# First attention pairs finished segment by segment, routing and low halves spread over a shared port, and two more raw buffers for early weight loads

## The chip, the cores and the metric

The kernel runs on one core of one Trainium2 chip. The metric is device time in microseconds (us) of one execution of the whole program, as the median of several runs. The core's engines are TensorE (PE in the rows, its weight loads PEld), VectorE (DVE), ScalarE (ACT), GpSimd (POOL) and SyncE (SP). Here SP does nothing but issue DMA transfers, in one fixed order.

## The reference

Attention with pooled queries feeds a mixture of experts with two experts for each row:

```
q_pool = q.reshape(B, H, S // 2, 2, D).mean(axis=3)      # B, H, S, D = 4, 8, 1152, 64
scores = matmul(q_pool, k.T) / sqrt(D)
attn   = exp(scores - max) / (sum + 1e-9)
x      = (attn @ v) laid out as 2304 rows of 512
noisy  = x @ w_gate + log1p(exp(x @ w_noise)) * noise    # 8 experts
top2   = the two largest of each row; weights = softmax of them
out    = sum over top2 of weight * (relu(x[mask] @ w1[e]) @ w2[e])   # 512 -> 1024 -> 512
```

All inputs and outputs are float32. The kernel keeps that precision by splitting numbers into a high and a low 16-bit half and multiplying the halves separately.

## The kernel before

**Attention.** The 32 heads (4 batches, 8 heads) are taken as 16 pairs. Each pair has 9 chunks of 128 queries, which make three segments of 3 chunks, so there are 48 segments. The score work is cut into 216 units `u` of two blocks of 128 keys by 384 queries. A unit goes through four engines: PE multiplies (`score`, L349 and L350), ACT takes the exponential (`exp`, L357), VectorE or GpSimd computes the low half of P (`p_lo`: one 128x768 instruction on VectorE, L362, or two of 128x384 on GpSimd, L365), and PE multiplies by V (`pv`, L385). Six P buffers (`pt`) connect these steps.

Before a pair's scores can run, its row maxima must be known. For each chunk PE makes two products against half of the keys (`max_mm`, L304), ACT takes a relu (L312), and VectorE a maximum (L318). For each segment a rest product and its maximum follow (`max_rest`, `rest_red`, L327). `max_fin` (three small VectorE instructions, L334 to L336) puts the negated maximum into two columns of `qn2`, and SP transposes `qn2` into `qt2` by DMA (L294). Pair 0 does this last step for each segment. All other pairs do it once, after their ninth chunk. The transposed queries `qt` (from `qn`) and keys `kt` (from `kn`) come by the same kind of DMA, and `kd` is a VectorE difference of transposed keys (L298).

**Routing.** The first half of the rows is complete when 8 pairs are done. Its routing (`Route.steps`) is a chain of PE logits (L693), some sixty small VectorE instructions on the tiles `rta` and `rua` (the softplus, the two largest, and the place of each row in its expert's list), and 18 scatters by GpSimd to `xg` in device memory (L97). The second half is routed in three parts when attention ends.

**Experts.** While attention ends, SP transposes 256 rows of each of the experts 0 and 1 out of `xg` (tile `xe`), and these are multiplied early (`Moe.early`). The weights come through four raw buffers that attention no longer needs (`kr`, `qr`, `kn`, `vr`); ACT and VectorE split them into halves (`split`, L918 and L920). From about 510 us on, the remaining products of all eight experts run (`Moe.run`).

**What sets the order.** Attention and the early products are written out by a list scheduler, class `Plan`. Every operation has an engine, a cost, a key (its due place, in blocks of attention), dependences and buffers. The scheduler takes, on the engine that can start first, the operation with the smallest key among those that start within `WIN` = 0.25 of the earliest. `port=True` keeps operations of VectorE and GpSimd from overlapping in the plan. The plan sets only the order of the instructions on each engine; on the chip they wait for each other by semaphores, and each engine, SP too, takes its instructions in that order.

Of the kernel before, what the change touches and what calls it, by code (L numbers as in the profile page):

```python
# [62 lines left out]
LATE = 440  # L63

# [47 lines left out]
class Plan:  # L112
# [64 lines left out]
    def run(s):  # L177
        while s.hard or s.holds:
            at = {}
            for o in s.can:  # L180
                b = s.start(o)
                if b is not None:
                    at.setdefault(b[1], []).append((b[0], o.key, o, b[2]))
            pick = None
            for e, c in at.items():
                m, _, _, cost = min(c, key=lambda x: (x[0], x[1]))
                lim = m + (WIN if s.soft else cost / 4)
                x = min((x for x in c if x[0] <= lim), key=lambda x: (x[1], x[0]))
# [12 lines left out]
            o.done = st + cost + (s.LAT[e] if o.lat is None else o.lat)  # L201
            s.now = st
            s.hard -= o.gen is None
            o.fn(e) if len(o.eng) > 1 else o.fn()
            for tag in o.give:
                s.end[tag] = max(s.end[tag], o.done)
                s.refs[tag] -= 1
                if not s.refs[tag]:
                    s.pools[s.home[tag]].append([s.end[tag], s.buf.pop(tag)])
            for x in o.succ:  # L210
                x.ready = max(x.ready, o.done)
            for x in o.succ + o.then:
                x.wait -= 1
                if not x.wait:
                    s.can.append(x)


class Attn:
# [95 lines left out]
    def max_red(s, i, c):  # L314
        if i not in s.mx:
            s.mx[i] = s.sm.tile([P, NCQ, 2], F32, name="mx")
        rd = s.G.buf["rd", i, c]
        s.nc.vector.tensor_tensor_reduce(out=rd, in0=s.G.buf["S", i, c], in1=rd, scale=1.0, scalar=-3.0e38,  # L318
                                         op0=ALU.add, op1=ALU.max, accum_out=s.mx[i][:, c, 0:1])

    def max_rest(s, i, g):
        kt, ps = s.G.buf["kt", i], s.G.buf["R", i, g]
# [86 lines left out]
    def pairs(s):  # L409
# [8 lines left out]
        for i in range(NPAIR):  # L418
# [16 lines left out]
            for h, c in enumerate(hs):  # L435
# [13 lines left out]
            for p in ((0, 1) if x else (2,)):  # L449
# [13 lines left out]
                t = op("SP", 1.35, k(43, 91) + 8 * p * x, lambda i=i, c=c: s.transpose(B["qt", i][:, c], B["qn", i][:, c]), deps=[hi], lat=2.7,  # L463
# [5 lines left out]
            allred = []  # L469
            for g in range(3):  # L470
# [14 lines left out]
                rest = op("PE", 0.39 if g == 1 else 0.17, k0 + 5, lambda i=i, g=g: s.max_rest(i, g), deps=red, take=[("bank", ("R", i, g))])  # L485
                red.append(op("DVE", 0.47, k0 + 7, lambda i=i, g=g: s.rest_red(i, g), deps=[rest], give=[("R", i, g)]))
                allred += red
                if x or g == 2:
                    c = slice(3 * g, 3 * g + 3) if x else slice(0, NCQ)
# [3 lines left out]
                           lat=3.0, take=[("qt2", ("qt2", i))] if g == 0 or not x else (), give=[("qn2", i)], after=ready[0, 0][0] if x and g else None)  # L493
                    for y in ((g,) if x else (0, 1, 2)):
# [12 lines left out]
        for u in range(NU):  # L507
# [5 lines left out]
            pls[u] = op((("POOL", 1.43), ("DVE", 0.87)), 0, 2 * u + 2, lambda eng, u=u: s.p_lo(u, eng), deps=[ex[u]], port=True)  # L513
        for n in range(NSEG):
            i, g = SEQ[n]
            done = []
            for kc in range(NK):
                t = n * NK + kc
                done.append(op("PE", 0.375 if g == 1 else 0.28, t + 8, lambda n=n, kc=kc: s.pv(n, kc), deps=[pls[t // 2]] + vdone[i], after=done[-1] if done else None,
# [6 lines left out]
    def others(s, F0, out):  # L526
# [3 lines left out]
        op("DVE", 1.2, 112, R.setup1, deps=[a], ready=30.0)  # L530
# [23 lines left out]
        s.route(R.steps(0, (0, 1, 2), R.A, 0.8), 245, [s.ev[i, g] for i in range(NH) for g in range(3)], 3.0, then=then, pace=0.8)  # L554
# [23 lines left out]
    def route(s, gen, key, deps, slack, soft=False, then=None, pace=0.0, first=("SP", 1.35)):  # L578
# [8 lines left out]
        def piece(bank, held):  # L587
# [9 lines left out]
            wait, eng, cost = d if isinstance(d, tuple) else (0.0, "DVE", 0.12 if soft else 0.3)  # L597
            ready = G.now + (0.24 if soft else 0.4) + wait + (slack if eng == "PE" else 0.0)
# [6 lines left out]
            else:  # L605
                add(eng, cost, ready=ready)
# [11 lines left out]
class Route:  # L618
# [14 lines left out]
    def setup0(s):  # L633
        nc = s.nc
        wg, wn, noise = s.args
# [5 lines left out]
        nc.gpsimd.iota(s.tok, pattern=[[P, 2 * NCQ]], base=1, channel_multiplier=1, allow_small_or_imprecise_dtypes=True)  # L641
        s.wf = s.wk.tile([P, 4, 2 * E], F32, name="wf", bufs=1)
# [56 lines left out]
    def steps(s, j, gs, tag, gap, L=None):  # L699
# [166 lines left out]
class Moe:  # L866
# [27 lines left out]
    def load(s, eng=None):  # L894
# [5 lines left out]
        r = s.B.flat(s.F0.raws[(s.nl - 1) % 4])  # L900
# [102 lines left out]
    def early(s, A):  # L1003
# [4 lines left out]
        s.W[0, "1"] = s.F0.w  # L1008
        fl, ld, done = {}, {}, {}
# [15 lines left out]
        for x, (e, nm) in enumerate(((0, "2"), (1, "1"), (1, "2"))):  # L1025
            for c in range(4):
                key = LATE + (2, 12, 24)[x] + (2, 2.5, 2.5)[x] * c
                hi = op("ACT", 1.06, key, lambda e=e, nm=nm, c=c: s.split(e, nm, c, 0), deps=[ld[x, c]] if x else ())
                lo = op("DVE", 1.14, key, lambda e=e, nm=nm, c=c: s.split(e, nm, c, 1, False), deps=[hi])
                last = ld[x + 1, c] = op("SP", 0.6, key, s.load, deps=[lo], lat=5.0, after=last)  # L1030
                done.setdefault((e, nm), []).append(lo)
        done[0, "1"] = [A.f0]
        for e in range(2):
# [178 lines left out]
```

## Time and profile before

| what | us |
|---|---|
| median of 3 runs (range) | 890.33 (889.83 to 892.76) |
| the profiled execution | 896.5 |
| its span in the trace | 894.6 |
| PE busy in the span | 819.0 (92%) |
| VectorE busy | 534.6 (60%) |
| ACT busy | 445.0 (50%) |
| GpSimd busy | 402.6 (45%) |

All times of rows come from the profiled execution. Attention ends at about 446 us, the early products run from there to about 510 us, and the main expert products from there to the end. Busy shares are averages over these stages, and they hide where one engine waits for another, so the rows below are read by stage. [...]

### The profile page before, as it was taken

Reading aid. Unit: us, or ns where it says so; the run is one execution under the profiler, and the core shown is the slowest. Engines: PE = TensorE matmul, PEld = TensorE weight load, DVE = VectorE, ACT = ScalarE, POOL = GpSimd, SP = SyncE. Lnnn points to the kernel's source line nnn. Section 1 sums busy time; section 2 is a strip of 40 time slices with the busy share of each in tenths; the row PEclk is TensorE's granted clock in tenths of the full one; section 3 lists DMA queues with packets and bytes.
Section 4 is the critical chain, followed back from the end, with each engine's and each line's share of the span. In section 5 each row is a group of like instructions: output and inputs, shape, how many; then the busy total and the mean of one; then the engine's idle time right before and its main releaser. Section 6 shows DMA issues by size and latency. Waiting matters only on the chain.

```text
span 894.6 us, 21128 instructions
## 1 busy us (share of the span) xinstructions
PE 819.0 (92%) x8685; PEld 537.1 (60%) x8685; DVE 534.6 (60%) x1226; ACT 445.0 (50%) x662; POOL 402.6 (45%) x389
## 2 busy tenths in 40 slices
PE   3889999999999877899988899999999999999995
PEld 1546777767767655677766365756475655647542
DVE  4877898899889988899887142434233241422200
ACT  4658888777878465586543132333233232322310
POOL 4447879887996867664633312020201102020222
PEclk9989999999999779899989899999999999999998
DMA  8899796898999587664586826282827346291143
GB/s 194 166 238 211 181 231 176 200 200 194 194 214 203 116 183 189 169 172 110 122 215 231 205 55 147 82 214 71 217 68 201 84 126 158 72 219 18 24 52 45
DMA packets 213637, 137.80 MB, mean 154 GB/s; under 512 B 150304, under 2 KB 183584, under 8 KB 213536
## 3 DMA queue, kind: packets, MB, share of 16 engines
q1 hardware_dynamic: 204896, 116.33, 53.6%
q0 software_dynamic: 8640, 20.08, 11.0%
q8 instruction: 69, 1.13, 0.5%
q14 instruction: 32, 0.26, 0.1%
HBM read 62.14 MB, written 35.44 MB: 109 GB/s over the span
## 4 chain that ended last, share of the span: by engine, by line
PE 64%; DVE 20%; issue 4%; ACT 4%; DMA 3%; another core or an unknown queue 1%; SPq 1%; POOL 1%; ACTq 0%; DVEq 0%; POOLq 0%
PE pss L971 23%; PE psm L988 21%; PE psm L385 7%; PE psm L304 5%; PE pss L350 4%; DVE pl L362 4%; PE pss L349 4%; DVE rd L318 3%; DVE kd L298 1%; ACT rd L312 1%; ACT pf L357 1%; DVE vv L288 1%; DVE mx L327 1%; DMA qt<-qn 1%
## 5 line engine op out<-in xcount | busy, mean ns | idle before, releaser
L365 POOL TENSOR_TENSOR pl<-pf 128x384 f16<-128x384 f32 x288 | 279.9, 1002 | 95.6 <-ACT pf L357 70.9
L357 ACT ACTIVATE pf<-pss 128x768 f32<-128x768 f32 x216 | 174.2, 813 | 72.1 <-PE pss L350 59.1
L97 POOL DMA_INDIRECT out_dram<-y,mti x40 | 62.2, 1554 | 317.4 <-ACT y L993 311.8
L385 PEld LDWEIGHTS <-pf 128*128 128x128 bf16 x2880 | 159.6, 99 | 52.8 <-issue 23.7
L385 PE MATMUL psm<-vv,pf 128*128 128x65 f16 (+1 forms) x2880 | 169.9, 196 | 6.0 <-ACT rd L312 3.2
L385 PE MATMUL psm<-vv,pl 128*128 128x65 f16 (+1 forms) x1440 | 161.1, 195 | 4.5 <-DVE pl L362 2.9
L349 PE MATMUL pss<-qt,kt 128*128 128x384 f16 (+1 forms) x576 | 152.1, 293 | 5.6 <-ACT pf L357 5.4
L350 PE MATMUL pss<-qt,kt 66*128 66x384 f16 (+1 forms) x576 | 152.6, 294 | 0.4 <-DMA qt<-qn 0.4
L981 DVE SCALAR_TENSOR_TENSOR hl<-pss,hh 128x640 f16<-128x640 f32 (+1 forms) x64 | 48.5, 758 | 158.9 <-ACT hh L980 158.9
L385 PEld LDWEIGHTS <-pl 128*128 128x128 f16 x1440 | 128.6, 100 | 6.1 <-DVE pl L362 3.4
L988 PE MATMUL psm<-wh,hh 128*128 128x512 f16 x320 | 122.5, 383 | 3.8 <-ACT hh L1015 3.8
L988 PE MATMUL psm<-wh,hl 128*128 128x512 f16 x320 | 122.3, 382 | 0.5 <-issue 0.5
L988 PE MATMUL psm<-wl,hh 128*128 128x512 f16 x320 | 122.5, 383 | 0.1
L318 DVE CUSTOM_DVE_ANT_0 rd<-psm,rd 128x512 f32<-128x512 f32 x144 | 97.3, 684 | 25.4 <-ACT rd L312 21.0
L988 PEld LDWEIGHTS <-hh 128*128 128x128 f16 x640 | 62.9, 98 | 79.8 <-ACT hh L1015 4.6
L993 ACT ACTIVATE y<-psm,mg 128x512 f32<-128x512 f32 x40 | 27.5, 688 | 152.0 <-issue 77.3
L980 ACT ACTIVATE hh<-pss 128x640 f16<-128x640 f32 (+1 forms) x64 | 41.7, 652 | 122.9 <-PE pss L971 122.9
L312 ACT ACTIVATE rd<-psm 128x512 f32<-128x512 f32 x144 | 85.9, 597 | 24.6 <-PE psm L304 19.7
L304 PE MATMUL psm<-kt,qt 128*128 128x512 f16 (+3 forms) x320 | 79.8, 325 | 16.4 <-DVE mx L318 8.7
L971 PE MATMUL pss<-xT,fh 128*128 128x320 f16 (+1 forms) x448 | 83.4, 303 | 0.0
L971 PE MATMUL pss<-xT,wh 128*128 128x320 f16 (+1 forms) x448 | 83.4, 303 | 0.0
L362 DVE TENSOR_TENSOR pl<-pf 128x768 f16<-128x768 f32 x72 | 82.0, 1151 | 0.2 <-ACT pf L357 0.2
(198 smaller groups left out, 1141.3 us busy)
## 6 DMA issues: line engine op xcount, KB each, us to landing
xg<-zt SPq DMA_DIRECT2D x40, 260.0 KB
kr<-in_k_dram SPq DMA_DIRECT2D x32, 288.0 KB
vr<-in_v_dram SPq DMA_DIRECT2D x16, 576.0 KB
kr<-in_moe_w_dram SPq DMA_DIRECT2D x17, 512.0 KB
qr<-in_moe_w_dram SPq DMA_DIRECT2D x16, 512.0 KB
kn<-in_moe_w_dram SPq DMA_DIRECT2D x16, 512.0 KB
qr<-in_q_dram SPq DMA_DIRECT2D x31, 256.0 KB
vr<-in_moe_w_dram SPq DMA_DIRECT2D x15, 512.0 KB
```

The costliest lines, as they stand in the source:

```text
L97: i = nc.gpsimd.indirect_dma_start(out=out, out_offset=bass.IndirectOffsetOnAxis(ap=idx, axis=0), in_=src, in_offset=None, **kw)
L304: s.nc.tensor.matmul(ps[r, o:o + m.shape[1] * P], s.G.buf["qt", i][:, c, r], m, start=True, stop=True)
L312: s.nc.scalar.activation(s.G.buf["rd", i, c], s.G.buf["D", i, c], AF.Relu)
L318: s.nc.vector.tensor_tensor_reduce(out=rd, in0=s.G.buf["S", i, c], in1=rd, scale=1.0, scalar=-3.0e38, op0=ALU.add, op1=ALU.max, accum_out= ...
L349: mm(ps[:, a, o:o + w], kt[:, hh * NK + kc, :], qf[:, q0:q0 + w], start=True, stop=False)
L350: mm(ps[:, a, o:o + w], kt2[0:66, hh * NK + kc, :], qf2[0:66, q0:q0 + w], start=False, stop=True)
L357: s.nc.scalar.activation(s.parts(u)[0], s.G.buf["ps", u][:, :, 0:SG], AF.Exp, scale=0.125 / (IN_SCALE * IN_SCALE))
L362: s.nc.vector.tensor_sub(pl, pf, ph)
L365: s.nc.gpsimd.tensor_sub(pl[:, a], pf[:, a], ph[:, a])
L385: mm(o[:, 0:x], src[:, t % 2, ci * P:ci * P + P], vv[:, hh * NK + kc, a:a + x], start=st, stop=last and src is pl, skip_group_check=True)
L971: nc.tensor.matmul(ps[:, i, 0:N], w[:, dc, f * P:(f + 1) * P], xT[:, 2 * dc + x, i * N:(i + 1) * N], start=(n == 0), stop=(n == 11))
L988: s.nc.tensor.matmul(ps, h[:, f, b * P:(b + 1) * P], w[:, f, :], start=(f == 0 and k == 0), stop=(f == 7 and k == 2))
```

## The change

It has three parts.

1. Pairs 1 to 3 also finish their maxima for each segment, which adds six times `max_fin` and the transposition of `qn2`. In pair 0 the first segment's rest product goes ahead of its other products and the second half of `kd` comes later. The three loads of the gate weights and the noise leave `setup0` and become an operation of their own on SP, `fetch`, which may start at 45 in the plan.
2. In the first half's routing the due places go from 245 with 0.8 for each piece to 290 with 1.0, VectorE's pieces are planned on the shared port, and scatters follow each other with a smaller gap. The low half of P is planned for each block of 128x384 by itself, on VectorE or GpSimd (`a` = 0, 1). The scheduler's pick becomes the smallest of start + 0.01 * key within 1.0.
3. The early products have six raw buffers: the fifth and sixth load (two chunks of W1 of expert 1) go to a tile `h` of the main products, which is allocated up front, and are issued at once. The second products' dependences in the plan become finer.

```diff
+KEY, PAC, SCW = 290, 1.0, 1.0
...
-                lim = m + (WIN if s.soft else cost / 4)
-                x = min((x for x in c if x[0] <= lim), key=lambda x: (x[1], x[0]))
+                lim = m + (1.0 if s.soft else cost / 4)
+                x = min((x for x in c if x[0] <= lim), key=(lambda x: (x[0] + 0.01 * x[1], x[0])) if s.soft else (lambda x: (x[1], x[0])))
...
-    def p_lo(s, u, eng):
-        pf, ph, pl = s.parts(u)
-        if eng == "DVE":
-            s.nc.vector.tensor_sub(pl, pf, ph)
-            return
-        for a in range(2):
-            s.nc.gpsimd.tensor_sub(pl[:, a], pf[:, a], ph[:, a])
+    def p_lo(s, u, a, eng):
+        pf, ph, pl = (x[:, a] for x in s.parts(u))
+        (s.nc.vector if eng == "DVE" else s.nc.gpsimd).tensor_sub(pl, pf, ph)
...
+            each = i < 4
...
+                soon = x and g == 0
+                rest = op("PE", 0.39 if g == 1 else 0.17, k0 + 5 - 6 * soon, lambda i=i, g=g: s.max_rest(i, g),
+                          deps=[q, tr[0]] if soon else red, take=[("wide" if soon else "bank", ("R", i, g))])
...
-                if x or g == 2:
-                    c = slice(3 * g, 3 * g + 3) if x else slice(0, NCQ)
+                if each or g == 2:
+                    c = slice(3 * g, 3 * g + 3) if each else slice(0, NCQ)
...
-                    for y in ((g,) if x else (0, 1, 2)):
+                    for y in ((g,) if each else (0, 1, 2)):
...
-            pls[u] = op((("POOL", 1.43), ("DVE", 0.87)), 0, 2 * u + 2, lambda eng, u=u: s.p_lo(u, eng), deps=[ex[u]], port=True)
+            pls[u] = [op((("POOL", 0.8), ("DVE", 0.47)), 0, 2 * u + 2 + a, lambda eng, u=u, a=a: s.p_lo(u, a, eng), deps=[ex[u]],
+                         port=True) for a in range(2)]
...
-        op("DVE", 1.2, 112, R.setup1, deps=[a], ready=30.0)
+        b = op("SP", 1.7, 100, R.fetch, lat=10.0, ready=45.0)
+        op("DVE", 1.2, 112, R.setup1, deps=[a, b])
...
-        s.route(R.steps(0, (0, 1, 2), R.A, 0.8), 245, [s.ev[i, g] for i in range(NH) for g in range(3)], 3.0, then=then, pace=0.8)
+        s.route(R.steps(0, (0, 1, 2), R.A, 0.8), KEY, [s.ev[i, g] for i in range(NH) for g in range(3)], 3.0, then=then, pace=PAC)
...
-            wait, eng, cost = d if isinstance(d, tuple) else (0.0, "DVE", 0.12 if soft else 0.3)
-            ready = G.now + (0.24 if soft else 0.4) + wait + (slack if eng == "PE" else 0.0)
+            wait, eng, cost = d if isinstance(d, tuple) else (0.0, "DVE", 0.12 if soft else 0.22)
+            ready = G.now + (0.24 if soft else 0.32) + wait + (slack if eng == "PE" else 0.0)
...
-                add(eng, cost, ready=ready)
+                add(eng, cost, ready=ready, port=eng == "DVE" and not soft)
...
-                yield (2.5 if j == 0 else 0.0, "POOL", 1.1) if gap else None
+                yield (SCW if j == 0 else 0.0, "POOL", 1.1) if gap else None
...
-        r = s.B.flat(s.F0.raws[(s.nl - 1) % 4])
+        if s.nl < 7:
+            r = s.H[1][1].rearrange("p a b -> p (a b)").bitcast(F32)[:, (s.nl - 5) * F:(s.nl - 4) * F]
+        else:
+            r = s.B.flat(s.F0.raws[(s.nl - 7) % 4])
...
+            for y in (4, 5, 6) if x == 0 else (x + 6,) if x < 4 else (x + 4,) if x > 5 else ():
+                last = ld[y] = op("SP", 0.6, key, s.load, deps=los[x:x + 1] if y > 5 else (), lat=5.0, after=last)
```

In the listings below, the number after a tile's name tells buffers apart; `kt_1` is a key tile of pair 1 and `qt2_0` the second query tile of pair 0.

SP's issues near the start, before, from the transposition of the first half of pair 0's keys on:

```order
L294 DMA_TRANSPOSE kt_0_94<-kn_73 128x9x128
L643 DMA wf_164<-in_moe_w_gate_dram 128x4x8
L644 DMA wf_164<-in_moe_w_noise_dram 128x4x8
L646 DMA nz_167<-in_moe_noise_dram 128x18x8
L294 DMA_TRANSPOSE kt_0_94<-kn_73 128x9x128
L294 DMA_TRANSPOSE qt_0_101<-qn_0_124 128x6x128
```

and of the change, from the same transpositions on:

```order
L295 DMA_TRANSPOSE kt_0_94<-kn_73 128x9x128 x2
L295 DMA_TRANSPOSE qt_0_101<-qn_0_124 128x6x128
L449 DMA kt2_0_121<-kt_0_94 64x1152 x2
L285 DMA vr_72<-in_v_dram 128x2x576
L266 DMA kr_70<-in_k_dram 128x576
```

The three loads of the gate weights and the noise (`wf`, `nz`) no longer stand between the two key transpositions, and the low halves of the keys (`kt2_0`) are copied before V is loaded.

A little later on SP, where pair 0's second query tile is finished and pair 1's queries and keys are transposed, before:

```order
L294 DMA_TRANSPOSE qt2_0_105<-qn2_0_126 128x3x128
L294 DMA_TRANSPOSE kt_1_95<-kn_73 128x9x128
L294 DMA_TRANSPOSE qt2_0_105<-qn2_0_126 128x3x128
L294 DMA_TRANSPOSE qt_1_102<-qn_1_125 128x9x128
L294 DMA_TRANSPOSE kt_1_95<-kn_73 128x9x128
L265 DMA kr_70<-in_k_dram 128x576 x2
L445 DMA kt2_1_122<-kt_1_95 64x1152
```

and of the change:

```order
L295 DMA_TRANSPOSE kt_1_95<-kn_73 128x9x128
L295 DMA_TRANSPOSE qt2_0_105<-qn2_0_126 128x3x128
L295 DMA_TRANSPOSE qt_1_102<-qn_1_125 128x9x128
L295 DMA_TRANSPOSE kt_1_95<-kn_73 128x9x128
L295 DMA_TRANSPOSE qt2_0_105<-qn2_0_126 128x3x128
L266 DMA kr_70<-in_k_dram 128x576
```

The queries of pair 1 (`qt_1`) and the second half of its keys (`kt_1`) are transposed ahead of the third part of `qt2_0`, no longer behind it.

VectorE in the first half's routing, at the six steps of the exponential (L746 before, L758 after; L362 and L369 are low halves of P, L318 and L317 the maxima of a chunk), before:

```order
L740 TENSOR_SCALAR rta<-rta 128x72
L743 TENSOR_SCALAR rta<-rta 128x72
L746 SCALAR_TENSOR_TENSOR rta<-rta 128x72 x6
L749 SCALAR_TENSOR_TENSOR rta<-rta 128x72
L752 TENSOR_SCALAR rta<-rta 128x72
L754 RECIPROCAL rta<-rta 128x72
L756 TENSOR_TENSOR rta<-rta 128x72
L759 TENSOR_TENSOR rta<-rta 128x72
L761 TENSOR_SCALAR rta<-rta 128x72
L763 TENSOR_SCALAR rta<-rua 128x72
L766 SCALAR_TENSOR_TENSOR rta<-rta 128x72 x5
L327 TENSOR_REDUCE mx<-psm_67 128x3
```

and of the change, where the same steps begin:

```order
L748 SCALAR_TENSOR_TENSOR rta<-rta 128x72
L289 SCALAR_TENSOR_TENSOR qn_0_126<-qs_100,qn_124 128x9x64
L750 SCALAR_TENSOR_TENSOR rta<-rta 128x72
L752 TENSOR_SCALAR rta<-rta 128x72
L369 TENSOR_TENSOR pl_114<-pf_113 128x384
L755 TENSOR_SCALAR rta<-rta 128x72
L369 TENSOR_TENSOR pl_114<-pf_113 128x384
L758 SCALAR_TENSOR_TENSOR rta<-rta 128x72
L317 ISA rd_107,mx<-psm_67,rd_107 128x512
L317 ISA mx 128x1
L317 ISA rd_108,mx<-psm_65,rd_108 128x512
L317 ISA mx 128x1
```

The routing instructions stood one behind the other. Now maxima, low halves of P and other work of attention stand between them. Over the whole program VectorE has 72 low halves of 128x768 before and 183 of 128x384 after, and GpSimd 288 of 128x384 before and 249 after.

## Rows read from the trace of the kernel before

**Rows 1.** Busy us by stretch: length, PE, PEld, DVE, ACT, POOL (instructions), clock, DMA, GB/s.

```profile
0.00:35.00 35.00, 17.22 (x76) 7.71 (x76) 20.09 (x48) 18.27 (x26) 13.58 (x20) 1.00 0.76 169
35.00:80.00 45.00, 39.46 (x507) 25.35 (x508) 37.16 (x87) 31.37 (x50) 23.34 (x24) 0.85 1.10 244
80.00:290.00 210.00, 201.11 (x3347) 152.21 (x3344) 187.55 (x429) 166.98 (x262) 177.51 (x181) 1.00 0.87 196
290.00:380.00 90.00, 72.63 (x1012) 52.05 (x1009) 78.99 (x198) 49.92 (x78) 65.31 (x73) 0.83 0.70 164
380.00:446.00 66.00, 61.28 (x1149) 50.05 (x1147) 60.63 (x110) 45.85 (x67) 40.44 (x35) 1.00 0.52 135
446.00:510.00 64.00, 53.67 (x413) 34.20 (x409) 40.18 (x186) 20.56 (x35) 22.72 (x22) 0.87 0.78 224
510.00:895.00 385.00, 373.65 (x2205) 215.54 (x2203) 110.00 (x170) 112.08 (x149) 59.74 (x39) 0.99 0.46 109
```

**Rows 2.** DMA issues on SP in order, 4 to 36 us: start, us, line, operation.

```profile
7.46 0.63 SPq L643 DMA_DIRECT2D wf<-in_moe_w_gate_dram  x1
...
9.32 2.17 SPq L294 DMA_TRANSPOSE kt<-kn  x1
...
24.06 1.21 SPq L294 DMA_TRANSPOSE qt<-qn  x1
...
29.39 2.58 SPq L294 DMA_TRANSPOSE qt<-qn  x2
```

**Rows 3.** Chain that ended last, 0 to 70 us: start, us, what.

```profile
22.69 1.05 ACT qn L291
...
30.67 4.29 DMA qt<-qn
...
35.01 1.89 PE psm L304 x4
...
59.83 4.08 DMA qt<-qn
```

**Rows 4.** VectorE in order, 12 to 36 us, idle time before in brackets.

```profile
13.48 0.43 DVE L298 TENSOR_TENSOR kd<-kt 128x512 f16<-128x512 f16 x1 [3.49 <-DMA kt<-kn]
...
28.78 0.17 DVE L334 TENSOR_REDUCE psm<-mx 128x3 f32<-128x6 f32 x1
...
29.20 0.17 DVE L336 SCALAR_TENSOR_TENSOR qn<-psm,qn 128x3 f16<-128x3 f32 x1
```

**Rows 5.** Tile rta (routing) alone: length, busy DVE, ACT, POOL, clock, DMA, GB/s.

```profile
290.00:322.00 32.00, 21.20 (x65) 0.20 (x1) 0.00 (x0) 0.83 0.60 143
```

**Rows 6.** VectorE in order, 290 to 308 us.

```profile
291.23 0.71 DVE L728 TENSOR_SCALAR rta<-rta 128x72 f32<-128x72 f32 x1
...
296.69 4.20 DVE L746 SCALAR_TENSOR_TENSOR rta<-rta 128x72 f32<-128x72 f32 x6
300.92 0.23 DVE L749 SCALAR_TENSOR_TENSOR rta<-rta 128x72 f32<-128x72 f32 x1
```

**Rows 7.** GpSimd in order, 290 to 304 us.

```profile
289.50 11.03 POOL L365 TENSOR_TENSOR pl<-pf 128x384 f16<-128x384 f32 x14
```

**Rows 8.** Exponentials (line 357) alone, 80 to 290 us: length, busy ACT (instructions).

```profile
80.00:290.00 210.00, 95.53 (x118) 1.00 0.87 196
```

**Rows 9.** VectorE in order, 346 to 369 us.

```profile
347.86 0.95 DVE L362 TENSOR_TENSOR pl<-pf 128x768 f16<-128x768 f32 x1
...
364.26 4.28 DVE L453 TENSOR_TENSOR qs<-qr 128x576 f32<-128x576 f32 x1
```

**Rows 10.** GpSimd in order, 356 to 372 us.

```profile
364.74 3.18 POOL L365 TENSOR_TENSOR pl<-pf 128x384 f16<-128x384 f32 x4
```

**Rows 11.** Scatters (line 97) of the first half: min/median/max ns, first and last start.

```profile
L97 POOL DMA_INDIRECT xg<-xa,rta x16: 972/990/1922, 323.3 to 388.0; - x16
```

**Rows 12.** SP's issues, 388 to 446 us.

```profile
397.63 2.28 SPq L671 DMA_TRANSPOSE xe<-xg  x1
```

**Rows 13.** Waits between 446 and 510 us: total, times, longest.

```profile
ACT wh L918 <- DMA vr<-in_moe_w_dram: 0.6, 1, 0.6
```

More of the change, by code (lines that the diff above doesn't have):

```diff
@@ L314, in max_red, with maxes, rest @@
     def max_red(s, i, c):
+        rd = s.G.buf["rd", i, c]
+        s.nc.vector.tensor_tensor_reduce(out=rd, in0=s.G.buf["S", i, c], in1=rd, scale=1.0, scalar=-3.0e38,
+                                         op0=ALU.add, op1=ALU.max, accum_out=s.maxes(i)[:, c, 0:1])
+    def maxes(s, i):
         if i not in s.mx:
             s.mx[i] = s.sm.tile([P, NCQ, 2], F32, name="mx")
-        rd = s.G.buf["rd", i, c]
-        s.nc.vector.tensor_tensor_reduce(out=rd, in0=s.G.buf["S", i, c], in1=rd, scale=1.0, scalar=-3.0e38,
-                                         op0=ALU.add, op1=ALU.max, accum_out=s.mx[i][:, c, 0:1])
+        return s.mx[i]
+    def rest(s, i, g):
+        ps = s.G.buf["R", i, g]
+        return ps[:, 0] if i == 0 and g == 0 else ps
     def max_rest(s, i, g):
-        kt, ps = s.G.buf["kt", i], s.G.buf["R", i, g]
+        kt, ps = s.G.buf["kt", i], s.rest(i, g)
         for ci in range(3):
@@ L331, in max_fin @@
         V = s.nc.vector
-        mx, qn2 = s.mx[i], s.G.buf["qn2", i]
-        m = s.G.buf["R", i, g][:, SG:SG + c.stop - c.start]
+        mx, qn2 = s.maxes(i), s.G.buf["qn2", i]
+        m = s.rest(i, g)[:, SG:SG + c.stop - c.start]
         V.reduce_max(m, mx[:, c], axis=AX.X)
@@ L492, in pairs @@
                     t = op("SP", 1.35, k0 + 9, lambda i=i, c=c: s.transpose(B["qt2", i][:, c], B["qn2", i][:, c]), deps=[fin],
-                           lat=3.0, take=[("qt2", ("qt2", i))] if g == 0 or not x else (), give=[("qn2", i)], after=ready[0, 0][0] if x and g else None)
-                    for y in ((g,) if x else (0, 1, 2)):
+                           lat=2.1 if x else 3.0, take=[("qt2", ("qt2", i))] if g == 0 or not each else (), give=[("qn2", i)], after=ready[i, 0][0] if each and g else None)
+                    for y in ((g,) if each else (0, 1, 2)):
                         ready[i, y] = [t] + [kc[h] for h in ((0,), (0, 1), (1,))[y]]
@@ L518, in pairs @@
                 t = n * NK + kc
[L519 removed]
+                done.append(op("PE", 0.375 if g == 1 else 0.28, t + 8, lambda n=n, kc=kc: s.pv(n, kc), deps=[pls[t // 2][t % 2]] + vdone[i], after=done[-1] if done else None,
                                take=[("bank", ("pv", n))] if kc == 0 else (), give=[("pt", t // 2), ("vv", i)]))
@@ L641, in setup0, with fetch @@
         nc.gpsimd.iota(s.tok, pattern=[[P, 2 * NCQ]], base=1, channel_multiplier=1, allow_small_or_imprecise_dtypes=True)
+    def fetch(s):
+        nc = s.nc
+        wg, wn, noise = s.args
         s.wf = s.wk.tile([P, 4, 2 * E], F32, name="wf", bufs=1)
@@ L1008, in early @@
         s.W[0, "1"] = s.F0.w
+        for e in range(2):
+            s.H[e] = tuple(s.h.tile([P, 8, CAP], F16, name=f"h{x}") for x in "hl")
         fl, ld, done = {}, {}, {}
@@ L1023, in one @@
             fl[e, f] = s.late.pop()
[L1025 to L1031, printed above, removed]
+        los = []
+        for x in range(12):
+            e, nm, c = s.loads[x]
+            key = LATE + (2, 12, 24)[x // 4] + (2, 2.5, 2.5)[x // 4] * c
+            hi = op("ACT", 1.06, key, lambda e=e, nm=nm, c=c: s.split(e, nm, c, 0), deps=[ld[x]] if x in ld else ())
+            los.append(op("DVE", 1.14, key, lambda e=e, nm=nm, c=c: s.split(e, nm, c, 1, False), deps=[hi]))
+            for y in (4, 5, 6) if x == 0 else (x + 6,) if x < 4 else (x + 4,) if x > 5 else ():
+                last = ld[y] = op("SP", 0.6, key, s.load, deps=los[x:x + 1] if y > 5 else (), lat=5.0, after=last)
+            done.setdefault((e, nm), []).append(los[-1])
         done[0, "1"] = [A.f0]
```

18 lines of the change are left out of this document (8 added, 10 removed).

## The prediction

> **What bounds the kernel now.** I read the view by stretches first [rows 1]: for each it shows how busy every engine is and what clock PE was granted. From 510 us to the end PE is busy 373.65 of 385 us at 0.99, and the change touches nothing there. From 80 to 290 us PE is busy 201.11 of 210 us, so attention's steady part loses only 4%, though VectorE at 187.55 us is close behind. PE waits in three other places: the first 80 us (17.22 of 35 us, then 39.46 of 45 us at a clock of 0.85), the stretch 290 to 380 us (72.63 of 90 us at 0.83), and the early products (53.67 of 64 us at 0.87). [...] So time can be won where PE starves, and part of each win is the clock.
>
> Then I read, for the start, SP's list of issues and the chain of waits [rows 2, 3], and for the routing the instructions of VectorE and GpSimd side by side [rows 5 to 7].
>
> **The start.** SP issues in order. Its second transposition of pair 0's keys starts at 9.32 us, behind three loads of gate weights and noise of which the first is issued at 7.46 us [rows 2]. VectorE sits idle 3.49 us until these keys land and it can form `kd` at 13.48 us [rows 4]. The change takes the loads away from there (9.32 - 7.46 = 1.9 us), and I count all of it: -1.9 (bounds 0 and -3.5, the whole wait). The loads come back near 45 us, where DMA's share is 1.10 and VectorE's use of them is due long after.
>
> The second wait is that of pair 1's queries. ACT has them ready at 22.69 + 1.05 = 23.74 us [rows 3]. But in SP's order they stand behind the third part of pair 0's second query tile, which needs VectorE's three small instructions ending at 29.37 us [rows 4]. SP waits for these and issues both transpositions from 29.39 us on [rows 2]; the queries land 4.29 us after their issue at 30.67 us, and PE's products for pair 1's maxima start at 35.01 us [rows 3]. In the new order they go before that third part. SP comes free at 24.06 + 1.21 = 25.3 us [rows 2], and 25.3 + 4.29 = 29.6 us is 5.4 us earlier: -5.4. Pair 0's scores are at work meanwhile, so what moves is the start of pair 1's nine chunks of maxima, for which everything up to 64 us then waits. Bounds: 0, if K or V loads are late instead (the DMA share is 1.10), and -7.
>
> Third, pair 1's scores wait for the second query tile, issued after all nine chunks: 59.83 + 4.08 = 63.9 us [rows 3]. With one finish per segment the first scores need three chunks of the nine. PE has 45 - 39.46 = 5.5 us of idle time in this stretch, and at 0.85 about 39.46 x 0.15 = 5.9 us go to the clock [rows 1]. That is 11.4 us in all; the 5.4 above draws on the same time. Half of the remaining 6 us: -3 (0 to -6). Sum of the start: -10.3, with bounds -1 and -16.
>
> The six added finishes cost VectorE 6 x 0.6 us (28.78 to 29.37 us [rows 4]) = 3.5 us, and SP six issues of 1.3 us each (two took 2.58 us [rows 2]). Most of it lies in the first 110 us beside PE's work: +0.5 (0 to +3.5).
>
> **The routing.** In the 32 us from 290 us on, `rta` alone holds VectorE for 21.20 us in 65 instructions [rows 5]. They are tiny, yet each takes 0.71 to 0.75 us while GpSimd runs low halves back to back (14 in 11.03 us, 0.79 each), and 0.23 us once GpSimd stops [rows 6, 7]. So each of them waits for a GpSimd instruction to end. They stand in one block, and behind them on VectorE stand the maxima and finishes of the next pairs; PE runs out of work.
>
> [...]
>
> What PE loses from 290 to 380 us: idle 90 - 72.63 = 17.4 us, and at a clock of 0.83 another 72.63 x 0.17 = 12.3 us [rows 1], in all 29.7. At the steady part's rate, 4% of some 60 us of work, 2.7 us would be lost anyway, so 27 us can be had. In the new order the pieces stand singly between maxima and low halves of P. Their demand on VectorE remains: 21.2 us at the contended price of 0.75, or 65 x 0.23 = 15 us without contention. They now spread over 26 units of scores. At the steady pace of one exponential, so one unit, in 210 / 118 = 1.78 us [rows 8] that is 46 us, in which VectorE has 11% spare (187.55 of 210 us busy), or 5 us. So 10 to 16 us stay over; I take 14, nearer the contended rows, since GpSimd keeps working beside them. Gain 27 - 14 = 13: -13. Bounds -25 (VectorE's other work shrinks when nothing piles up) and -5 (one more collision for every piece, 22 us lost).
>
> **The low halves.** VectorE gets 183 of 128x384 in place of 72 of twice the size, 39 more halves; one costs 0.95 / 2 = 0.48 us [rows 9], together 18.5 us. GpSimd sheds 39 x 0.79 = 31 us [rows 7]. By the order, 24 of them fall after 290 us and 18 between 80 and 290 us (three go the other way at the start). In the steady part that makes 187.55 + 18 x 0.48 = 196 us on VectorE, still under PE's 201 [rows 1], and GpSimd falls from 177.5 us by 14. Halves also release PE's product after one block instead of two. Both signs are possible: +0.5 (-4 to +6).
>
> **The early products.** Of the waits between 446 and 510 us only 0.6 us is for a weight load [rows 13], so earlier loads have nothing to win at once; PE's order there is the same. One of the new loads stands on SP ahead of the last three transpositions of attention's rows, and waits for attention's last P products to free `hl`'s place: 0 (-3 to +3).
>
> The first half's rows go out later. Sixteen recorded scatters run from 323.3 to 388.0 us, 0.99 us each [rows 11], and SP fetches the early rows at 397.63 us [rows 12], almost 50 us before they are needed. In the new order the scatters lie at units 185 to 202 of 216 and the fetch at unit 209, which leaves 7 x 1.78 = 12 us. I count 0 for it.
>
> [...]
>
> **Sum.** -10.3 + 0.5 - 13 + 0.5 + 0 = -22.3 us on the profiled execution's 896.5 us (span 894.6): 874.2 us. That execution lay 6.2 us above the median of 890.33, so I predict 874.2 - 6.2 = 868 us.
>
> **Rivals.**
> - VectorE becomes the bound after 290 us, and only the start gains. For it: VectorE is busy 78.99 + 60.63 = 139.6 us of 156 from 290 to 446 us [rows 1], and 24 halves add 11.5 us. Against it: its time there is swollen by waits for GpSimd [rows 6, 7]. 890.3 - 10 = 880 us. Chance 0.19.
> - More is won: the routing all but disappears (-25) and the start gives -13. For it: 27 us of PE's time can be had there, and GpSimd's load falls by 31 us. Against it: 15 us of VectorE work must go somewhere. 852 us. Chance 0.14.
> - Slower: VectorE is the bound from 80 to 446 us. The 18.5 us of halves and 3.5 us of finishes all land on the end, and the routing costs as before: 22 - 10.3 = +11.7, so 902 us. This decides once VectorE's busy share passes PE's in the steady part (now 187.55 against 201.11, and 196 by my sum). Chance 0.08.
> - The rows of the first half come too late. Were each of 18 scatters to take the longest time seen, 1.92 us [rows 11], that adds 18 x 0.93 = 16.7 us on GpSimd against 12 us of room: +5, 873 us, within my own range. If scatters and fetch keep today's place in time while attention ends 22 us earlier, nothing is won: 890 us. Chance 0.07.
>
> **How the numbers follow.** My case has 0.52, with a range of its own of 860 to 877 us. Less than 0.3% (2.7 us) can't be told from no change by a measurement of this kernel. Faster: 0.52 + 0.19 + 0.14 and 0.01 of the last = 0.86; same 0.05; slower 0.09. Leaving out the slower case, most of the last one and the far end of the second gives 850 to 887 us.
>
> **What would show it.** In the profile after: `kd` of pair 0 near 11.6 us and pair 1's first maxima products near 30 us; pair 1's first scores before 58 us; PE's clock over 0.9 and no long idle time from 290 to 380 us; attention's last product near 424 us; the same 64 us for the early products, with no wait for `xe`. I am wrong if VectorE is busy over 95% of the steady part while PE waits for low halves or maxima, or if the early products wait for rows.

## The result and the profile after

The changed kernel takes 898.56 us (median of 6 runs, 895.16 to 902.90) against 892.24 us before in the same sessions (889.83 to 893.69). The ratio is 1.0068, with a 95% interval of 1.0045 to 1.0091. It is 0.7% slower, where I had forecast 868 us.

The view by stretches of the changed kernel, with the columns of [rows 1]:

```profile
0.00:35.00 35.00, 18.42 (x110) 9.52 (x111) 26.46 (x65) 20.17 (x31) 15.96 (x22) 0.95 0.84 205
35.00:80.00 45.00, 42.77 (x691) 32.31 (x689) 42.29 (x101) 36.41 (x56) 36.69 (x37) 0.96 0.95 209
80.00:290.00 210.00, 193.04 (x3048) 142.25 (x3045) 200.16 (x459) 157.74 (x247) 147.04 (x148) 1.00 0.81 190
290.00:380.00 90.00, 75.11 (x1196) 55.96 (x1193) 87.18 (x228) 57.49 (x90) 49.21 (x50) 0.98 0.67 151
380.00:446.00 66.00, 54.29 (x907) 42.76 (x907) 57.40 (x138) 38.79 (x58) 35.56 (x33) 0.95 0.56 162
446.00:510.00 64.00, 54.76 (x545) 37.35 (x542) 45.66 (x193) 22.55 (x38) 19.66 (x20) 0.95 0.78 219
```

From 80 to 290 us VectorE was busy 187.55 us before [rows 1] and is busy 200.16 us now, while PE fell from 201.11 to 193.04. VectorE's share is now above PE's, the point at which my third rival decides. The clock is the share of its full clock that PE was granted; taken for each us by itself it is 1.00 in 56, 0.50 in 26 and between them in 8 of the 90 us from 290 to 380 us before. In two of the other stretches where PE had starved it rose: 0.96 in place of 0.85 from 35 to 80 us, and 0.98 in place of 0.83 from 290 to 380 us. In two more it fell, from 1.00 to 0.95: 0 to 35 us and 380 to 446 us.

PE's waits for low halves of P between 80 and 446 us (total us, times, longest), before:

```profile
PE psm L385 <- DVE pl L362: 2.9, 4, 1.1
```

and after:

```profile
PE psm L389 <- DVE pl L369: 12.8, 19, 1.7
```

The chain that ended last, share of the span by engine, before:

```profile
PE 64%; DVE 20%; issue 4%; ACT 4%; DMA 3%; another core or an unknown queue 1%; SPq 1%; POOL 1%; ACTq 0%; DVEq 0%; POOLq 0%
```

and after:

```profile
PE 54%; DVE 32%; issue 6%; DMA 3%; ACT 2%; POOL 2%; SPq 1%; DVEq 0%; ACTq 0%; POOLq 0%
```

VectorE's part of the chain rose from 20% to 32%. To see where the time went, I read off when the exponential of a unit starts, and when attention's last product with V ends (us; e1 to e9 are the experiments below):

| | unit 27 | unit 135 | unit 189 | last PV | span |
|---|---|---|---|---|---|
| before | 89.8 | 282.8 | 405.6 | 446.0 | 894.6 |
| after | 72.8 | 283.3 | 401.0 | 453.1 | 897.1 |
| e1, whole low halves | 83.0 | 279.6 | 381.3 | 429.4 | 876.3 |
| e2, e1 with the whole ones split | 81.7 | 284.6 | 390.4 | 440.7 | 886.8 |
| e4, start alone | 75.2 | 272.7 | 395.1 | 435.5 | 881.8 |
| e6, routing alone | 87.9 | 278.7 | 388.2 | 439.0 | 883.6 |
| e7, halves alone | 94.3 | 298.8 | 420.4 | 464.3 | 910.7 |
| e9, halves on GpSimd | 73.4 | 291.8 | 402.5 | 459.0 | 900.7 |

Each row is one execution. That of the kernel before took 896.5 us, 4 us more than its median, and e1 and e8 (below), in which PE has the same order throughout, start unit 27 at 83.0 and 77.9 us; so a difference of 5 us in this table tells little by itself.

The start won 17 us by unit 27. The steady part from unit 27 to 135 took 210.5 us instead of 193.0 and gave all of it back. From unit 135 to 189, where the routing lies, 5 us were won, and the tail took 52.1 us instead of 40.4.

The low halves of P on VectorE in the costliest groups (busy us, mean ns of one), before:

```profile
L362 DVE TENSOR_TENSOR pl<-pf 128x768 f16<-128x768 f32 x72 | 82.0, 1151 | 0.2 <-ACT pf L357 0.2
```

and of the changed kernel, on both engines:

```profile
L369 POOL TENSOR_TENSOR pl<-pf 128x384 f16<-128x384 f32 x249 | 244.4, 1002 | 138.2 <-ACT pf L365 116.5
...
L369 DVE TENSOR_TENSOR pl<-pf 128x384 f16<-128x384 f32 x183 | 137.1, 784 | 0.1
```

Two halves on VectorE now take 2 x 784 = 1568 ns, where one whole low half of the kernel before had a mean of 1151 ns. VectorE's low halves went from 82.0 us (72 of them) to 137.1 us: 55 us more, where my sum had 18.5. Why one costs so much is seen in the order of time. GpSimd, from 157.12 us on:

```profile
157.12 2.89 POOL L369 TENSOR_TENSOR pl<-pf 128x384 f16<-128x384 f32 x3
```

and VectorE beside it:

```profile
159.25 1.18 DVE L369 TENSOR_TENSOR pl<-pf 128x384 f16<-128x384 f32 x1
```

This half starts at 159.25 us, the third GpSimd instruction ends at 157.12 + 2.89 = 160.01 us, and the half ends at 160.43 us, 0.42 us later. Near attention's end, where GpSimd is idle when it starts, the same instruction takes 0.55 us:

```profile
440.55 0.55 DVE L369 TENSOR_TENSOR pl<-pf 128x384 f16<-128x384 f32 x1
...
443.73 0.55 DVE L369 TENSOR_TENSOR pl<-pf 128x384 f16<-128x384 f32 x1
```

Counted over the program by whether a GpSimd instruction was running at the start, 106 halves took 0.96 us on average and 77 took 0.55. In the kernel before, 31 whole ones took 1.42 us beside GpSimd and 41 took 0.95 alone. The mean wait is 1.42 - 0.95 = 0.47 us for a whole one and 0.96 - 0.55 = 0.41 us for a half: it hardly shrinks with the size, and two halves can wait twice (in e2 below 92 of 150 halves start beside GpSimd, in e1 54 of 75 whole ones). The runs show this wait and not what makes it; the shared port is a rule of the plan. Two halves alone also take 2 x 0.55 - 0.95 = 0.15 us more than a whole one alone.

GpSimd, relieved of 39 halves, now waits for exponentials instead. In the stretch 80 to 290 us (total us, times, longest), before:

```profile
POOL pl L365 <- ACT pf L357: 24.0, 18, 4.4
```

and after:

```profile
POOL pl L369 <- ACT pf L365: 54.0, 46, 4.6
```

### The profile page after: what moved, and what is told of

The parts are those of the page before. It is cut to its first block, busy times and chain, and to the rows that moved or that the text cites. A ratio compares the mean times of both kernels' runs of the same rounds, so it can differ in the third digit from the quotient of the medians.

```text
span 897.1 us, 21225 instructions
## 1 busy us (share of the span) xinstructions
PE 812.7 (91%) x8685; PEld 536.1 (60%) x8685; DVE 569.9 (64%) x1356; ACT 444.8 (50%) x662; POOL 366.5 (41%) x349
## 4 chain that ended last, share of the span: by engine, by line
PE 54%; DVE 32%; issue 6%; DMA 3%; ACT 2%; POOL 2%; SPq 1%; DVEq 0%; ACTq 0%; POOLq 0%
PE pss L986 22%; PE psm L1003 20%; DVE pl L369 9%; DVE rd L317 6%; PE psm L389 5%; PE psm L305 2%; PE pss L357 2%; PE pss L358 2%; DVE mx L335 2%; DVE kd L299 2%; DVE kn L289 2%; DVE vv L289 1%; POOL xg L98 1%; DVE psm L402 1%; ACT pf L365 1%
## 5 line engine op out<-in xcount | busy, mean ns | idle before, releaser
L369 POOL TENSOR_TENSOR pl<-pf 128x384 f16<-128x384 f32 x249 | 244.4, 1002 | 138.2 <-ACT pf L365 116.5
L389 PE MATMUL psm<-vv,pf 128*128 128x65 f16 (+1 forms) x2880 | 173.2, 196 | 9.7 <-DVE vv L289 3.2
L357 PE MATMUL pss<-qt,kt 128*128 128x384 f16 (+1 forms) x576 | 149.0, 288 | 10.2 <-ACT pf L365 10.2
L358 PE MATMUL pss<-qt,kt 66*128 66x384 f16 (+1 forms) x576 | 149.7, 290 | 0.0
L369 DVE TENSOR_TENSOR pl<-pf 128x384 f16<-128x384 f32 x183 | 137.1, 784 | 0.1
L317 DVE CUSTOM_DVE_ANT_0 rd<-psm,rd 128x512 f32<-128x512 f32 x144 | 97.0, 681 | 2.6 <-ACT rd L313 1.2
L305 PE MATMUL psm<-kt,qt 128*128 128x128 f16 (+3 forms) x317 | 75.2, 309 | 11.8 <-DVE mx L317 6.6
```

Of the source, the lines that this page charges most:

```text
L305: s.nc.tensor.matmul(ps[r, o:o + m.shape[1] * P], s.G.buf["qt", i][:, c, r], m, start=True, stop=True)
L357: mm(ps[:, a, o:o + w], kt[:, hh * NK + kc, :], qf[:, q0:q0 + w], start=True, stop=False)
L358: mm(ps[:, a, o:o + w], kt2[0:66, hh * NK + kc, :], qf2[0:66, q0:q0 + w], start=False, stop=True)
L369: (s.nc.vector if eng == "DVE" else s.nc.gpsimd).tensor_sub(pl, pf, ph)
L389: mm(o[:, 0:x], src[:, t % 2, ci * P:ci * P + P], vv[:, hh * NK + kc, a:a + x], start=st, stop=last and src is pl, skip_group_check=True)
```

## The experiments

Each kernel was timed in turns with the kernel before; ratios stand with 95% intervals. Theory A: VectorE's low halves in half-size pieces each wait for their own GpSimd instruction, and made VectorE the bound. Theory B: the scheduler's new pick costs. Theory C: the steady part is bound by something else, and any lead of the start is lost there.

**e1.** The change with whole low halves:

```diff
-            pls[u] = [op((("POOL", 0.8), ("DVE", 0.47)), 0, 2 * u + 2 + a, ... for a in range(2)]
+            pls[u] = op((("POOL", 1.43), ("DVE", 0.87)), 0, 2 * u + 2, lambda eng, u=u: s.p_lo(u, eng), deps=[ex[u]], port=True)
```

> The changed kernel, but the low half of P is planned per unit of 128x768 again (one VectorE instruction, or two on GpSimd); all else as changed. Theory A (each VectorE instruction on the shared port waits for its own GpSimd instruction, so 183 halves at 0.78 us in place of 72 of 1.15 us made VectorE the bound of the steady part, 200 of 210 us busy): VectorE has about 75 of them at 1.15 us, is busy near 188 of 210 us again, the start's lead of 17 us at unit 27 stays, total 874 to 882 us. Theory B (the scheduler's new pick is what costs): still 894 to 900 us. Theory C (the start's lead is always lost, since attention's steady part is bound by something the start does not change): 888 to 894 us, with the lead at unit 135 under 4 us.

Measured: 877.27 us, ratio 0.9825 (0.980 to 0.985). One edit turns 0.7% slower into 1.8% faster. VectorE's low halves in e1:

```profile
L370 DVE TENSOR_TENSOR pl<-pf 128x768 f16<-128x768 f32 x75 | 93.2, 1258 | 0.4 <-ACT pf L365 0.3
```

and the stretches around the routing:

```profile
80.00:290.00 210.00, 197.33 (x3199) 148.60 (x3199) 192.42 (x432) 163.43 (x256) 179.66 (x180) 1.00 0.86 194
290.00:380.00 90.00, 81.89 (x1402) 62.02 (x1399) 85.15 (x245) 66.66 (x102) 63.51 (x65) 1.00 0.79 173
```

VectorE at 192.42 us is under PE's 197.33 again, and PE's clock is 1.00 from 290 to 380 us, through the routing. The total is inside theory A's range. The lead at unit 27 was only 6.8 us in this execution, not the 17 expected, and 3.2 at unit 135; units 135 to 189 took 101.7 us instead of 122.8.

**e2.** e1 in the same order on every engine, with VectorE's whole instruction issued as two:

```diff
-        if eng == "DVE":
-            s.nc.vector.tensor_sub(pl, pf, ph)
-            return
+        e = s.nc.vector if eng == "DVE" else s.nc.gpsimd
         for a in range(2):
-            s.nc.gpsimd.tensor_sub(pl[:, a], pf[:, a], ph[:, a])
+            e.tensor_sub(pl[:, a], pf[:, a], ph[:, a])
```

> The kernel of e1 in the same order on every engine, but where VectorE has a low half of 128x768 it now issues two instructions of 128x384. Theory A: the two together take about 2 x 0.78 = 1.57 us instead of 1.15 us, 75 x 0.4 = 30 us more of VectorE's time, and most of the gain of e1 goes: 884 to 895 us. Theory B and C: the same as e1 within 3 us, since order and number of elements are the same.

Measured: 889.00 us, ratio 0.9971 (0.9951 to 0.9991), 11.7 us slower than e1 in the same session. Order and elements are the same; only the number of VectorE instructions differs:

```profile
L371 DVE TENSOR_TENSOR pl<-pf 128x384 f16<-128x384 f32 x150 | 114.9, 813 | 1.2 <-ACT pf L365 1.1
```

```profile
80.00:290.00 210.00, 194.73 (x3120) 145.23 (x3120) 195.10 (x442) 160.30 (x251) 169.01 (x177) 1.00 0.83 191
```

75 whole ones of 1.258 us (93.2 us) became 150 of 0.813 us (114.9 us). This is the cleanest pair: splitting alone costs 11.7 us. Theory A is only a part of why. Added up by duration, the low halves on VectorE take 122.0 us instead of 94.4. Of these 27.6 us, 75 x 0.15 = 11 are the longer time of two halves alone, and the other 16.6 are waits for GpSimd: 92 halves start beside a running GpSimd instruction, where 54 whole ones did. The 11.7 us were not divided between the two.

**e3.** The change with the old pick:

```diff
-                lim = m + (1.0 if s.soft else cost / 4)
+                lim = m + (WIN if s.soft else cost / 4)
```

> The changed kernel with the scheduler's old pick (smallest key within 0.25 of the earliest start); low halves stay per block of 128x384. Theory A: VectorE keeps 182 halves and stays the bound, 893 to 902 us. Theory B: 875 to 884 us. Theory C: 888 to 896 us.

Measured: 900.81 us, ratio 1.0120 (1.008 to 1.016). Theory B falls: with the old pick the time does not come down.

**e4.** The kernel before with the first part alone:

```diff
+            each = i < 4
...
+        b = op("SP", 1.7, 100, R.fetch, lat=10.0, ready=45.0)
```

> The kernel before with the first part of the change alone (pairs 1 to 3 finish per segment, rest product of pair 0 ahead, loads of gate and noise later, its shorter latencies in the plan). Theory A: the lead of some 17 us at unit 27 is kept through the steady part, 875 to 882 us. Theory B: the same. Theory C: lead lost by unit 135, 888 to 894 us.

Measured: 886.62 us, ratio 0.9938 (0.9914 to 0.9961). That lies between the ranges of theories A and C. The profiled execution leads by 14.6 us at unit 27, 10.1 at unit 135 and 10.5 at the last PV, so a lead of the start is not always lost, as theory C has it. The median moved less, 6 us: the profiled execution is the fastest of its runs, and that of the kernel before is 4 us slower than its median. The routing's hole is as before:

```profile
80.00:290.00 210.00, 199.53 (x3346) 151.52 (x3346) 186.45 (x427) 163.61 (x254) 185.62 (x190) 1.00 0.92 204
290.00:380.00 90.00, 71.50 (x941) 49.82 (x941) 77.18 (x210) 52.62 (x83) 64.71 (x69) 0.85 0.69 169
```

**e5.** e1 with the old pick as well, the edit of e3.

> The changed kernel with low halves per unit (as e1) and the old pick too: the start, the routing and the six buffers are left of the change. If the new pick costs something by itself (e1's exponentials at unit 135 are only 3.2 us ahead of before, those of the start alone 10.1 us): lead at unit 135 near 10 us, routing gain of 21 us kept, 865 to 872 us. If it costs nothing: 875 to 880 us. If it helps: over 880 us.

Measured: 881.85 us, ratio 0.9894 (0.986 to 0.993). The median is in the third case, that the new pick helps; the runs spread from 874.9 to 886.1. The lead at unit 135 was 5 us. Against e1's 0.9825 the pick is worth 5 to 6 us beside whole low halves.

e3 and e5 are a second pair that differs in the low halves alone, both with the old pick: 1.0120 against 0.9894, or 20 us. With e1 against the changed kernel (21 us) and e7 below (19 us), planning the low halves one by one costs about the same whatever stands beside it.

**e6.** The kernel before with the routing's part alone (its smaller costs in the plan and its scatter gap go with it, not shown here):

```diff
-        s.route(R.steps(0, (0, 1, 2), R.A, 0.8), 245, ..., 3.0, then=then, pace=0.8)
+        s.route(R.steps(0, (0, 1, 2), R.A, 0.8), 290, ..., 3.0, then=then, pace=1.0)
...
-                add(eng, cost, ready=ready)
+                add(eng, cost, ready=ready, port=eng == "DVE" and not soft)
```

> The kernel before with the routing's new due places, costs, shared port and scatter gap alone. If routing spread out is what won 21 us between units 135 and 189 in e1: these units take 100 to 105 us instead of 122.8, 870 to 878 us in total. If VectorE's load after 290 us gives it back in the tail (units 189 to 215 took 42 us in e1, 36 before): 878 to 884 us. If it needs the other parts: 887 to 894 us.

Measured: 885.67 us, ratio 0.9945 (0.993 to 0.996).

```profile
290.00:380.00 90.00, 78.40 (x1262) 59.45 (x1263) 79.83 (x233) 60.03 (x92) 53.82 (x55) 0.94 0.73 162
380.00:446.00 66.00, 56.05 (x1045) 46.02 (x1042) 59.27 (x116) 39.47 (x59) 34.39 (x28) 1.00 0.71 163
```

PE gets 78.40 of 90 us at 0.94, against 72.63 at 0.83 before [rows 1]. Units 135 to 189 took 109.5 us, 13.3 less than before, but the tail from there to the last PV took 50.8 us, 10.4 more: most of the gain is given back there, and the total reaches none of the three ranges.

**e7.** The kernel before with the low halves per block alone, the reverse of e1's edit.

> The kernel before with the low halves planned per block of 128x384 alone (176 on VectorE). Theory A: each half takes 0.55 us alone and 0.95 us when GpSimd is running (a whole one 0.95 and 1.39 us), so VectorE's low halves cost 135 to 140 us instead of 82, and its share of the steady part goes to 0.94 to 0.96: 903 to 914 us. If halves hurt only together with the pick: 888 to 898 us.

Measured: 910.44 us, ratio 1.0212 (1.018 to 1.024), as theory A has it.

```profile
L361 DVE TENSOR_TENSOR pl<-pf 128x384 f16<-128x384 f32 x176 | 134.6, 794 | 0.8 <-ACT pf L357 0.7
```

```profile
80.00:290.00 210.00, 194.08 (x3133) 145.76 (x3130) 199.00 (x449) 159.96 (x250) 142.80 (x147) 0.99 0.77 180
```

By itself this edit costs 19 us; VectorE goes to 199.00 us and PE falls to 194.08.

**e8.** e1 with the four raw buffers of before, and with the second products' dependences of before, so without the third part of the change.

> e1 with the old four raw buffers in the early products. If six buffers win nothing, as I forecast (0, bounds -3 and 3): 874 to 881 us. If the 5 us by which the changed kernel's stage from attention's last product to the end was shorter than before (444.0 against 448.6 us) are theirs: 880 to 884 us.

Measured: 876.13 us, ratio 0.9843 (0.982 to 0.987). The third part wins nothing, and 444.0 against 448.6 us from the last PV to the end is not their doing.

**e9, e10 and e12** move low halves from VectorE to GpSimd by the plan's price, in the changed kernel (e9, e12) and in e1 (e10):

```diff
-            pls[u] = [op((("POOL", 0.8), ("DVE", 0.47)), ...
+            pls[u] = [op((("POOL", 0.8), ("DVE", 0.7)), ...      # e9; 0.49 in e12
...
-            pls[u] = op((("POOL", 1.43), ("DVE", 0.87)), ...
+            pls[u] = op((("POOL", 1.43), ("DVE", 1.15)), ...     # e10
```

> The changed kernel with one number of the plan raised: a half of P on VectorE is reckoned at 0.7 instead of 0.47 (0.78 is the mean measured). The plan then puts 19 halves on VectorE and 413 on GpSimd. Theory A (what costs is VectorE's port work in small pieces): VectorE's share of the steady part falls under 0.85, and the time goes under 890 us unless GpSimd, with 413 x 0.82 = 339 us in the 425 us of attention beside its scatters, becomes the bound itself: 872 to 888 us. If halves are bad on either engine (one release per half, whoever computes it): 895 to 905 us.

> e1 with a whole low half on VectorE reckoned at 1.15 (the measured mean before) instead of 0.87: 13 whole ones on VectorE, 406 halves on GpSimd. If the balance of e1 (75 on VectorE) is right: slower than e1, 882 to 895 us, GpSimd busy over 0.9 of the steady part. If VectorE is still too full in e1 (192 of 210 us): 866 to 874 us.

> The changed kernel with a half of P on VectorE reckoned at 0.49 instead of 0.47: the plan puts 96 halves on VectorE and 336 on GpSimd (before: 72 wholes and 288, e2: 150 and 282). Splitting alone, with the order kept, cost 11.7 us (e2 against e1); the changed kernel lies 9.6 us above e2, and 33 more halves are on VectorE there. If VectorE's load is what makes these 9.6 us: 96 x 0.78 = 75 us of low halves, VectorE at about 0.85 of the steady part, 876 to 886 us. If the order that comes from planning halves one by one costs by itself (e9 against e10, 15 us with hardly a low half on VectorE): 890 to 902 us.

Measured: e9 906.18 us, ratio 1.0172 (1.011 to 1.023); e10 891.26 us, ratio 0.9991 (0.997 to 1.002); e12 906.62 us, ratio 1.0163 (1.011 to 1.022). Theory A alone wanted e9 and e12 under 890 us; it missed both. VectorE does have room in e9:

```profile
80.00:290.00 210.00, 190.36 (x2975) 140.34 (x2974) 156.67 (x389) 155.83 (x244) 187.21 (x208) 1.00 0.90 199
```

and the wait that grew is another one. In the stretch 80 to 446 us the exponentials wait for PE's products with V (total us, times, longest). Before:

```profile
ACT pf L357 <- PE psm L385: 3.3, 5, 1.7
```

in the changed kernel:

```profile
ACT pf L365 <- PE psm L389: 26.6, 32, 2.7
```

in e9:

```profile
ACT pf L365 <- PE psm L389: 68.3, 77, 2.5
```

in e12:

```profile
ACT pf L365 <- PE psm L389: 35.1, 42, 2.5
```

in e10:

```profile
ACT pf L365 <- PE psm L393: 39.8, 48, 5.1
```

and in e1:

```profile
ACT pf L365 <- PE psm L393: 15.0, 20, 1.8
```

The six P buffers hold 12 blocks. In the order of these programs PE's scores stand on average (leaving out the start and the end of attention) 14.0 blocks ahead of its products with V in e9, 12.3 in e12, 12.4 in e10, 11.7 in the changed kernel, 10.8 in e1 and e2 and 9.8 before. Where scores run over 12 blocks ahead the P buffers are full, and ACT waits for PE to work off products that stand later in PE's order. In e9 this fits the time: units 27 to 135 took 218.4 us, with VectorE far from full. But it is read from the order and the wait, and no edit isolates it; nor does it come from halves alone, since e10, with whole low halves, has as much of it as e12 (39.8 and 35.1 us, 12.4 and 12.3 blocks) and is 15 us faster. Why e12 takes 906 us stays open. e7 (10.0 blocks, 1.0 us of this wait) shows that halves are slow without it.

**e11.** e1 with the routing's due place at 265 instead of 290.

> e1 with the routing's due place at 265 instead of 290. In e1 units 189 to 215 took 42 us, 36 before, with VectorE at 59 of 66 us from 380 us on. If late routing fills VectorE in the tail: tail near 38 us, 870 to 875 us. If not: 875 to 880 us.

Measured: 884.26 us, ratio 0.9915 (0.990 to 0.993), above both ranges. The later place is better. The expectation that late routing fills the tail fails: units 189 to 215 take 42 us in both, while units 135 to 189 take 111.1 us instead of 101.7.

## Why the prediction was wrong

The step that failed is the one on the low halves: "one costs 0.95 / 2 = 0.48 us [rows 9], together 18.5 us", with the value +0.5 and bounds -4 to +6. The edit alone costs 19 us (e7), and taking it out of the change wins 21 (e1). Two things in that step were wrong. I halved the price of an instruction that ran without GpSimd beside it, 0.95 us, though a half alone takes 0.55 us. And I let a price without waits stand for all of them, though I had read in [rows 6, 7] that an instruction of 128x72 took 0.71 us beside GpSimd's low halves and 0.23 us after them; the mean of whole ones over the program was 1.151 us. With 0.784 us measured, the changed kernel's low halves hold VectorE 55 us longer, and the room I saw (196 us against PE's 201) was gone. From 80 to 290 us alone they hold it for 58.1 us instead of 33.6, where my sum had 9 us more.

Added up by duration, where ends that overlap count twice, it is 61 us (183 x 0.784 against 72 x 1.151), in three parts: the 18.5 of my sum; 13 because each of 183 halves takes 0.55 us alone and not 0.475; and 29 of waits, 106 x 0.41 = 43 us in place of 31 x 0.47 = 15.

Of the 21 us, 11.7 are shown to come from splitting (e2). The other 9.6 were not separated: the changed kernel has 33 halves more on VectorE than e2, and its scores stand further ahead (11.7 against 10.8 blocks). In e7 there are 32 halves more than in the kernel before and the scores are hardly further ahead (10.0 against 9.8), and it loses 19 us; that speaks for VectorE's load.

The sign of being wrong that I had named came: VectorE is busy 200.16 of 210 us, 95.3%, and PE waits 12.8 us for its low halves instead of 2.9. Attention's last product came at 453.1 us, not near 424.

Point by point:
- The start: right in mechanism, too large in size, with 10.3 us forecast. `kd`'s second half comes at 11.05 us, the forecast being 11.6. `qt_1` goes out as the second of the two issues from 20.34 us on instead of at 30.67, and pair 1's first maxima products come at 25.87 us instead of 35.01, the forecast being 30:

```profile
9.58 0.42 DVE L299 TENSOR_TENSOR kd<-kt 128x512 f16<-128x512 f16 x1 [1.44 <-DMA kt<-kn]
...
11.05 0.42 DVE L299 TENSOR_TENSOR kd<-kt 128x512 f16<-128x512 f16 x1
```

```profile
20.34 2.58 SPq L295 DMA_TRANSPOSE qt<-qn  x2
```

```profile
25.87 0.38 PE L305 MATMUL psm<-kd,qt 128*128 128x512 f16 x1
```

  By itself it won 10.5 us of attention in the profiled execution and 6 us in the median (e4). In the changed kernel its 17 us at unit 27 were gone by unit 135.
- The routing: 13 us forecast. In the changed kernel units 135 to 189 gained 5 us. Alone it won 13.3 us there and gave 10.4 back in the tail (e6), 5.5 us in the median; beside the start and whole low halves units 135 to 189 gained 21 us, and the tail lost 8 (e1). Its demand remained, as I had reckoned, but my "21.2 us at the contended price of 0.75" is a misreading: 65 pieces at 0.75 us are 49 us, and 21.2 us are 0.33 each, some beside GpSimd and some not. Spread out they took 0.27 us each; `rta` by itself in the changed kernel (length, busy DVE, ACT, POOL, clock, DMA, GB/s):

```profile
330.00:360.00 30.00, 10.38 (x21) 0.00 (x0) 0.00 (x0) 0.94 0.46 126
360.00:400.00 40.00, 9.02 (x50) 0.21 (x1) 7.56 (x7) 0.96 0.53 136
```

- The early products: 0 forecast. The third part wins nothing (e8).
- The scatters: 0 forecast, and PE waits for no early row. They run until 417.0 us with a median of 1.11 us, against 0.99 [rows 11]:

```profile
L98 POOL DMA_INDIRECT xg<-xa,rta x18: 969/1110/2046, 387.6 to 417.0; - x18
```

  PE does wait 2.9 us for the rows of the main products, which it did not before; e7, with the old routing, shows 4.8 us of this wait, so the later scatters are not needed for it:

```profile
PE pss L986 <- DMA xT<-xg: 2.9, 1, 2.9
```

  What made the scatters 0.12 us longer was not shown by any run.
- The rivals: the third, VectorE as the bound from 80 to 446 us, is what came, at 898.6 us instead of 902. I gave it 0.08. It gave the routing no gain and the halves 18.5 us; in truth the routing gained and the halves cost far more, so that its number came so near is luck.

The parts nearly add up: -6 (start) -5.5 (routing) -5 (pick, uncertain) is about e1's -15.4 us. With the 19 us of e7, measured by itself, that makes +4, where +6 was measured. So the low halves turned a gain into a loss. Of the 23 us forecast without them e1 has 15, and about 5 of these are the pick's, to which my sum gave no term; the start and the routing were both put too high.

e1 and e8, at 876 to 877 us, beat both kernels: the change without its planning of low halves one by one.

## What to carry to other kernels

Here a low half on VectorE that started beside a running GpSimd instruction cost its own time plus a wait that hardly shrank with its size (0.47 us for a whole one, 0.41 for a half), and cutting 75 of them in two added 38 waits and 0.15 us for each cut (e2). So price halves by a row measured beside the other engine, and compare the sum with what the bounding engine has left. A lead won early can be lost where an engine fills up behind it: 17 us here, with VectorE at 95%. Mending one price of a list scheduler does not mend its order: with a half on VectorE reckoned at 0.49 and at 0.7 us instead of 0.47, the time was 906 us both times (e12, e9).

## What was not expected

One number of the plan moved the low halves in jumps: VectorE's price of a half at 0.47, 0.49 and 0.7 puts 183, 96 and 19 of them there, and none of the three kernels is faster than before. And e10, with 13 whole low halves on VectorE in place of 75, frees over 30 us of VectorE in the steady part (160.4 against 192.4 us busy) and is still 14 us slower than e1: GpSimd is then busy 203.91 of the 210 us:

```profile
80.00:290.00 210.00, 197.26 (x3166) 149.05 (x3164) 160.43 (x392) 162.32 (x253) 203.91 (x220) 0.98 0.87 203
```
